# A retention layer and a leaky-ReLU MLP on one core: one load handed from GpSimd to SyncE, a smaller limit on GpSimd's loads under way, and two pairs of casts placed ahead of later loads

## The chip, the core and the metric

The kernel runs on one core of a Trainium2 chip. The time is device microseconds of one launch, from a median of eight runs; lower is better. One further execution was taken with the hardware profiler, and every duration below comes from that one.

## What is computed

The first stage is causal retention over a batch of 8, 8 heads, 576 positions and a head size of 64, and the second is a two-layer MLP on its output. The reference, cut to what matters:

```python
scores = scale * np.matmul(q, k.transpose(0, 1, 3, 2))
Dmat = np.where(rel >= 0, gamma ** rel, 0.0)        # per head, rel = i - j
ret = np.matmul(scores * Dmat, v)
x = ret.transpose(0, 2, 1, 3).reshape(4608, 512)    # tokens x model
h = x @ w_in                                        # 512 x 2048
out = np.maximum(0.01 * h, h) @ w_out               # 2048 x 512
```

All inputs and the output are float32; the kernel multiplies in float16 and accumulates in float32.

## The kernel before

**Units.** The 4608 tokens are cut into 36 units of 128 tokens (two chunks of 64). For each unit the kernel loads q, k and v (256 KB each; three tags of a pool with five buffers, `t32_0`, `t32_1`, `t32_2`), casts them to float16, transposes q and k, multiplies k by q and k by v per head (`scores`, L209), masks (`masks`, L232), carries a running state in float32 (`states`, L241), and puts together the unit's output (`outputs_acc`, L280, for units 0 to 3; `outputs`, L313, after that) in `xT`. A load of a unit that spans two batch entries is two transfers of 128 KB (unit 4 is one).

**Who casts.** `cast_k` (L155) is on ScalarE. `scaled` (L159) puts q and v on VectorE for units 0 to 5 and on GpSimd from unit 6 on. From unit 7 on (`NPE = 7`) `cast_q` also has SyncE issue a DMA transpose of the cast q and k (L171); before that TensorE transposes (`transposes`, L187).

**MLP.** The tokens of two units make a group g. Its first layer is eight blocks of eight 256-column matmuls (L455), each block followed by a leaky ReLU on ScalarE (L462) that frees one of two PSUM buffers `hps`. The second layer is 512-column matmuls (L523 for groups 0 and 1 together, the "wide" blocks; L478 afterwards). VectorE or ScalarE copies the result to one of four buffers `osb`, and SyncE stores it (L490, L534).

**Order.** Each engine runs its instructions in program order; the order is written by hand from L543 to L656, then the units go on as `steps` of the loop (`steady`, L406), spread between the blocks of the MLP by `run` (L498). In `steady(n)` SyncE loads unit n+6 and unit n+3 is cast. Up to unit 11 the loads are issued by GpSimd, except k and q of unit 0, which SyncE issues. So GpSimd's queue holds, in this order: v of unit 0, units 1 to 3, the eight halves of `w_in` (512 KB in HBM each, cast to float16 by the DMA), `w_out` quarter 0 (1 MB in HBM), unit 4, `w_out` quarter 1, unit 5, `w_out` quarters 2 and 3, units 6 to 9, casts of unit 6, load of unit 10, casts of unit 7, load of unit 11, casts of units 8 to 11.

**The limit.** `ring` (L128) keeps a list of GpSimd's transfers with their size in HBM. Before a transfer that would bring the listed sum over `RING` (13 x 256 KB), GpSimd copies one element of the oldest listed transfer's destination into a scratch tile (`probe`, L132); this copy waits for that transfer to land, and GpSimd waits with it. Apart from that, the framework gives GpSimd's DMAs eight completion semaphores in turn, and the ninth DMA waits on the first's; the DMAs of SyncE and ScalarE together have eight more, used the same way.

Names used below: k10 is the load of k of unit 10; T7 is SyncE's DMA transpose for unit 7; w_out(2) is the third quarter of `w_out`.

Of the kernel before, what the change touches and what calls it, by code (L numbers as in the profile page):

```python
# [17 lines left out]
def kernel(  # L18
# [23 lines left out]
    nc = tc.nc  # L42
# [7 lines left out]
    NF = DFF // P  # L50
    TOK = 512
    XR = NT // 2
    RING = 13 << 18

    gamma = 1.0 - 2.0 ** (-5.0 - np.arange(H, dtype=np.float64))
    scale = 1.0 / np.sqrt(D)
# [71 lines left out]
    def ring(size, at):  # L128

        while landing and sum(n for n, _ in landing) + size > RING:  # L130
            x = landing.pop(0)[1]
            nc.gpsimd.tensor_copy(out=probe[0:1, 0:1], in_=x)  # L132
        landing.append((size, at))
# [4 lines left out]
    def load(u, x, eng):  # L138
        t = ld_pool.tile([P, H, D], FP, name=f"t32_{x}")
        t32[u, x] = t  # L140
        (b0, c0), (b1, c1) = units[u]
        src = (q, k, v)[x]
        parts = [(t, b0, c0, P)] if b0 == b1 else [(t[0:CH], b0, c0, CH), (t[CH:P], b1, c1, CH)]
        for dst, b, c, n in parts:
            if eng is nc.gpsimd:
                ring(H * n * D * 4, dst[0:1, 0, 0:1])
            eng.dma_start(  # L147
                out=dst, in_=src[b, :, CH * c : CH * c + n, :].rearrange("h t d -> t h d")
            )

    def loads(u, eng):
        for x in (1, 0, 2):
            load(u, x, eng)

    def cast_k(u):  # L155
        qk16[u] = b_pool.tile([P, 2, H, D], F16, name="qk16")
        nc.scalar.copy(out=qk16[u][:, 1], in_=t32[u, 1])  # L157
# [9 lines left out]
    def cast_q(u):  # L167
        scaled(u, 0, qk16[u][:, 0])
        if u >= NPE:
            qkT[u] = b_pool.tile([P, 2, NP, P], F16, name="qkT")  # L170
            nc.sync.dma_start_transpose(  # L171
                out=qkT[u].rearrange("p x c t -> p (x c) t"),
                in_=qk16[u].rearrange("t x h d -> t (x h d)"),
            )

    def cast_v(u):
        v16[u] = b_pool.tile([P, H, D], F16, name="v16")
        scaled(u, 2, v16[u])

    def casts(u):  # L180
        if u >= NU:
            return
        cast_k(u)
        cast_q(u)
        cast_v(u)

    def transposes(u, pool=None):  # L187

        qkT[u] = b_pool.tile([P, 2, NP, P], F16, name="qkT")
        if pool is None:  # L190
            trs = [y_pool.tile([P, NP, P], F16, name="yps") for x in range(2)]
        else:
            both = pool.tile([P, 2, 2 * NP, P], F16, name="sc" if pool is sc_pool else "ot")
            trs = [both[:, x, 0:NP, :] for x in range(2)]
        for x in (1, 0):
            for p in range(NP):
                nc.tensor.transpose(
                    trs[x][:, p, :],
                    qk16[u][:, x, 2 * p : 2 * p + 2, :].rearrange("t h d -> t (h d)"),
                    ident,  # L200
                )
        for x in (1, 0):
            (nc.scalar.copy if x or u < 4 else nc.vector.tensor_copy)(
                out=qkT[u][:, x], in_=trs[x]
            )
# [185 lines left out]

    load(0, 1, nc.sync)
    load(0, 0, nc.sync)
    load(0, 2, nc.gpsimd)
    for u in (1, 2, 3):
        loads(u, nc.gpsimd)
    for c in range(4):
# [200 lines left out]
    def some(a, b):  # L598
        for m in range(a, b):
            wide[m]()  # L600
# [3 lines left out]
    def more(blocks, a, b):  # L604
        for m in range(a, b):
            blocks[m]()
# [15 lines left out]
    states(5)  # L622
    loads(9, nc.gpsimd)
    casts(6)
    some(9, 12)
    loads(10, nc.gpsimd)
    casts(7)
    some(12, 13)
    outputs(5)
    some(13, 16)  # L630
    more(g1[2], 0, 1)
    transposes(6, sc_pool)
    loads(11, nc.gpsimd)
    casts(8)
    more(g1[2], 1, 3)
    scores(6)
    masks(6)
# [67 lines left out]
```

## Time and profile before

| | us |
|---|---|
| median of 8 runs | 306.11 |
| lowest and highest run | 303.77, 307.25 |
| the profiled execution | 306.61 |
| its span, first to last instruction | 304.7 |
| TensorE busy | 291.7 (96%) |
| ScalarE, GpSimd, VectorE busy | 138.0, 123.2, 107.0 |

The profiled execution is 1.9 us longer than its span, and 0.5 us longer than the median of the runs. The page of the profile gives the busy share of each engine in 40 slices of 7.6 us, the groups of instructions, the DMA queues (q0 is GpSimd's, q1 is SyncE's), and the chain of work that ended last, followed back from the end. The timeline of an engine lists its instructions with start, duration and the idle time ahead of each, with what ended that idle time.

### The profile page before, as it was taken

How to read it: one execution, taken by the hardware profiler on the slowest of the kernel's cores; microseconds unless marked ns; L12 is line 12 of the kernel's file. 1: busy time of each engine (PE TensorE's matmuls, PEld its weight loads, DVE VectorE, ACT ScalarE, POOL GpSimd, SP SyncE). 2: the span in 40 equal slices, each digit the busy share in tenths (PEclk: the TensorE clock that was granted, in tenths of full speed). 3: DMA queues.
4: the chain of work that ended last, by engine and by line, in shares of the span. 5: the costliest groups of instructions: out<-in, count | busy, mean ns of one | idle time of the engine just before them, and what ended most of it. 6: DMA issues, size and time to landing. Idle time of an engine off the chain costs nothing.

```text
span 304.7 us, 9480 instructions
## 1 busy us (share of the span) xinstructions
PE 291.7 (96%) x4169; PEld 197.2 (65%) x4169; DVE 107.0 (35%) x200; ACT 138.0 (45%) x240; POOL 123.2 (40%) x177
## 2 busy tenths in 40 slices
PE   3989999998899999999999999999999999999996
PEld 3467755846666666666666666666666666666663
DVE  2760144344442425242524243433333234331001
ACT  3676634844554445353535353535353534343320
POOL 8986989972533333333333333333333330000000
PEclk9999999999999999999999999999999999999999
DMA  8999998998899999968496957685797221000111
GB/s 223 262 189 238 203 253 268 226 197 197 195 205 199 263 212 198 199 168 199 131 183 163 216 141 177 169 184 160 156 174 189 73 69 39 34 37 34 39 66 69
DMA packets 120440, 50.26 MB, mean 165 GB/s; under 512 B 109264, under 2 KB 113744, under 8 KB 120400
## 3 DMA queue, kind: packets, MB, share of 16 engines
q1 hardware_dynamic: 112912, 36.38, 54.0%
q0 software_dynamic: 7056, 13.11, 18.4%
q8 instruction: 32, 0.52, 0.8%
q10 hardware_dynamic: 432, 0.17, 0.3%
q14 instruction: 8, 0.07, 0.1%
HBM read 36.81 MB, written 9.44 MB: 152 GB/s over the span
## 4 chain that ended last, share of the span: by engine, by line
PE 71%; DMA 12%; POOL 9%; issue 4%; SPq 2%; ACT 0%; POOLq 0%; ACTq 0%
PE yps L478 33%; PE hps L455 32%; DMA w_out<-in_moe_w_out_dram 5%; POOL t L147 5%; DMA t<-in_v_dram 3%; PE sc L216 2%; DMA w_in<-in_moe_w_in_dram 2%; DMA qkT<-qk 2%; POOL probe L132 1%; SPq L147 1%; PE ot L323 1%; PE yps L665 1%; PE ot L334 1%; DMA t<-in_k_dram 1%; PE sc L225 1%
## 5 line engine op out<-in xcount | busy, mean ns | idle before, releaser
L455 PE MATMUL hps<-xT,w_in 128*128 128x256 f16 x1152 | 146.2, 273 | 2.5 <-ACT gt L462 1.4
L462 ACT ACTIVATE gt<-hps 128x512 f16<-128x512 f32 x144 | 85.7, 597 | 125.9 <-PE hps L455 125.6
L455 PEld LDWEIGHTS <-w_in 128*128 128x128 f16 x1152 | 112.1, 98 | 40.7 <-issue 3.1
L478 PE MATMUL yps<-w_out,gt 128*128 128x512 f16 x496 | 126.3, 380 | 0.0
L268 POOL CAST st<-s 128x512 f16<-128x512 f32 (+1 forms) x28 | 15.6, 557 | 138.5 <-DVE s L255 54.9
L478 PEld LDWEIGHTS <-gt 128*128 128x128 f16 x496 | 46.3, 98 | 34.3
L346 DVE TENSOR_TENSOR xT<-ot,own 128x512 f16<-128x512 f32 x32 | 22.1, 692 | 80.0 <-ACT own L342 80.0
L488 DVE COPY osb<-yps 128x512 f32<-128x512 f32 x31 | 21.3, 687 | 75.4 <-PE yps L478 75.4
L160 POOL TENSOR_TENSOR v<-t,cs 128x512 f16<-128x512 f32 x30 | 31.3, 1042 | 1.2 <-DMA t<-in_v_dram 1.2
L160 POOL TENSOR_TENSOR qk<-t,cs 128x512 f16<-128x512 f32 x30 | 31.3, 1043 | 0.7 <-DMA t<-in_q_dram 0.5
L234 DVE TENSOR_TENSOR s<-sc,cs 128x512 f16<-128x512 f32 x36 | 24.6, 683 | 8.2 <-PE sc L225 8.2
L157 ACT CAST qk<-t 128x512 f16<-128x512 f32 x36 | 22.2, 621 | 5.3 <-DMA t<-in_k_dram 5.3
L342 ACT COPY own<-ot 128x512 f32<-128x512 f32 x32 | 18.8, 586 | 7.1 <-PE ot L334 5.2
L255 DVE TENSOR_TENSOR s<-sc,s 128x256 f32<-128x256 f32 x40 | 16.8, 420 | 0.7
L216 PEld LDWEIGHTS <-qkT 64*64 64x64 f16 x576 | 7.8, 108 | 11.9 <-issue 7.3
L216 PE MATMUL sc<-qkT 64*64 64x64 f16 x576 | 11.6, 199 | 2.4 <-DVE s L255 1.2
L147 POOL DMA_DIRECT2D t<-in_v_dram x13 | 11.3, 868 | 1.0 <-POOLq L689 0.8
L147 POOL DMA_DIRECT2D t<-in_k_dram x12 | 10.4, 865 | 1.7 <-ACT gt L462 1.7
L225 PE MATMUL sc<-v,qk 64*64 64x64 f16 x576 | 10.9, 194 | 0.1
L147 POOL DMA_DIRECT2D t<-in_q_dram x12 | 10.2, 853 | 1.2 <-DMA t<-in_k_dram 1.2
L523 PEld LDWEIGHTS <-gt 128*128 128x128 f16 x64 | 5.9, 98 | 6.3
L323 PE MATMUL ot<-s,v 64*64 64x64 f16 x512 | 9.8, 194 | 0.0
(52 smaller groups left out, 145.4 us busy)
## 6 DMA issues: line engine op xcount, KB each, us to landing
out_dram<-osb SPq DMA_DIRECT2D x35, 256.0 KB, 3.8
t<-in_k_dram SPq DMA_DIRECT2D x22, 256.0 KB, 3.6
t<-in_q_dram SPq DMA_DIRECT2D x22, 256.0 KB, 4.1
t<-in_v_dram SPq DMA_DIRECT2D x21, 256.0 KB, 4.5
t<-in_v_dram POOLq DMA_DIRECT2D x11, 256.0 KB, 5.4
t<-in_k_dram POOLq DMA_DIRECT2D x10, 256.0 KB, 4.9
t<-in_q_dram POOLq DMA_DIRECT2D x10, 256.0 KB, 5.4
w_in<-in_moe_w_in_dram POOLq DMA_DIRECT2D x8, 256.0 KB, 6.1
```

The costliest lines, as they stand in the source:

```text
L147: eng.dma_start(out=dst, in_=src[b, :, CH * c : CH * c + n, :].rearrange("h t d -> t h d"))
L157: nc.scalar.copy(out=qk16[u][:, 1], in_=t32[u, 1])
L160: (nc.vector if u < NEARLY else nc.gpsimd).tensor_tensor(out=out, in0=t32[u, x], in1=tab_sb[:, kind(u), x // 2, :].unsqueeze(2).to_broadca ...
L216: nc.tensor.matmul(out=a[half(j), g, 0, p, :], lhsT=qkT[u][half(g), 1, p, half(j)], rhs=qkT[u][half(g), 0, p, half(j)], start=True, stop=T ...
L234: nc.vector.tensor_tensor(out=s16s[u], in0=sc_tiles[u][:, :, 0], in1=mask_sb.unsqueeze(1).unsqueeze(1).to_broadcast([P, 2, NP, CH]), op=MUL,)
L255: nc.vector.tensor_tensor(out=dst, in0=st[:, j], in1=prev, op=ADD)
L342: nc.scalar.copy(out=tmp.rearrange("q c (j t) -> q c j t", t=CH), in_=own.rearrange("q j c t -> q c j t"),)
L346: nc.vector.tensor_tensor(out=xT[:, :, t0 : t0 + P].rearrange("q (s g) t -> q g s t", g=2), in0=far, in1=tmp.rearrange("q (s g) t -> q g s ...
L455: nc.tensor.matmul(out=hps[:, f, :], lhsT=w_in16[:, c, fc * P : (fc + 1) * P], rhs=xT[:, c, t0 % XR : t0 % XR + tok], start=(c == 0), stop ...
L462: nc.scalar.activation(out=g_tiles[g][:, fb * nf : (fb + 1) * nf, :], in_=hps, func=mybir.ActivationFunctionType.Lrelu,)
L478: nc.tensor.matmul(out=y_cur[g, tb], lhsT=g_tiles[g][:, f, tb * P : (tb + 1) * P], rhs=w_out16[:, f, :], start=(f == 0), stop=(f == NF - 1),)
L488: nc.vector.tensor_copy(out=osb, in_=y_cur[g, tb])
```

## The change

There are three edits. `RING` goes from 13 to 10 times 256 KB. The load of v of unit 0 is issued by SyncE, after k and q of the same unit, and is no longer in GpSimd's list. The casts of unit 7 stand ahead of the load of unit 10, and the casts of unit 8 ahead of the load of unit 11.

```diff
-    RING = 13 << 18
+    RING = 10 << 18
...
     load(0, 1, nc.sync)
     load(0, 0, nc.sync)
-    load(0, 2, nc.gpsimd)
+    load(0, 2, nc.sync)
...
     loads(9, nc.gpsimd)
     casts(6)
+    casts(7)
     some(9, 12)
     loads(10, nc.gpsimd)
-    casts(7)
     some(12, 13)
...
     transposes(6, sc_pool)
+    casts(8)
     loads(11, nc.gpsimd)
-    casts(8)
     more(g1[2], 1, 3)
```

The order of instructions on TensorE, VectorE and ScalarE is the same in both kernels. On SyncE one load is added in the third place. On GpSimd the first load is gone, the probes stand in other places, and eight instructions (four casts, with the loads around them) change places.

## The prediction

> **What bounds the kernel now.** I read the page's slices first, then the list of TensorE's waits, then the timelines of SyncE and GpSimd where those waits fall.
>
> ```profile
> span 304.7 us, 9480 instructions
> PE 291.7 (96%) x4169; PEld 197.2 (65%) x4169; DVE 107.0 (35%) x200; ACT 138.0 (45%) x240; POOL 123.2 (40%) x177
> ...
> PE   3989999998899999999999999999999999999996
> ...
> POOL 8986989972533333333333333333333330000000
> ...
> DMA  8999998998899999968496957685797221000111
> ```
>
> TensorE is full from slice 11 (84 us) to the end, and GpSimd works hard in the first 12 slices alone. Whatever the change does, it does it before about 88 us; after that TensorE runs on at its own pace and the end moves as that point moves. So the sum is a shift of TensorE's work at 80 to 88 us. What TensorE waits for:
>
> ```profile
> PE yps L197 <- DVE qk L160: 1.7, 1, 1.7
> PE yps L197 <- ACT qk L157: 1.6, 1, 1.6
> PE hps L455 <- ACT gt L462: 1.4, 2, 1.1
> PE hps L387 <- DVE idle L375: 1.4, 1, 1.4
> PE sc L216 <- DVE s L255: 1.2, 1, 1.2
> PE hps L455 <- issue: 1.1, 1, 1.1
> PE sc L216 <- ACT qkT L203: 0.7, 1, 0.7
> PE sc L216 <- DMA qkT<-qk: 0.5, 1, 0.5
> ```
>
> The columns are the total, the count and the longest. 6.5 us of this lies before 25 us (k0, q0, the start, one issue gap, unit 2's transposes). Between 60 and 80 us there are four waits of 3.0 us in all: 0.32 at 60.28 (ScalarE's leaky ReLU), 0.48 at 68.33 (T8), 1.16 at 74.33 (VectorE's state of unit 9) and 1.07 at 79.02 (a leaky ReLU that stands behind ScalarE's cast of k13, which waits for that load). The last one ends last. The chain of waits leads from it to k13's load (issued 74.40, landed 77.70), and from there back along SyncE's queue:
>
> ```profile
> 54.72 1.32 SPq L171 DMA_TRANSPOSE qkT<-qk  x1
> 56.08 3.02 SPq L534 DMA_DIRECT2D out_dram<-osb  x4
> 59.76 10.04 SPq L171 DMA_TRANSPOSE qkT<-qk  x4
> 69.92 0.51 SPq L147 DMA_DIRECT2D t<-in_k_dram  x1
> ```
>
> The columns are the start and the duration. T7 waits for GpSimd's cast of q7 (53.63 to 54.68). The four stores stand behind it, though the first one's data was ready at 49.92. T8 starts as q8's cast ends (59.74); then T8 to T11 follow each other with no gap (2.91, 2.95, 2.06, 1.63 us) and the loads of units 12 and 13 come behind them. So what counts is **when T11 leaves SyncE**: 68.18. The chain puts GpSimd's cast of v11 ahead of it, but T10 and T11 need the casts of q10 and q11 only, which were done at 63.7 and 65.7; SyncE was simply busy.
>
> **Edit 1, v0 on SyncE.** GpSimd's first issue (1.24 to 2.29) goes, and its next loads start 1.05 earlier. SyncE issues v0 at about 1.8, behind q0. q0's last packets ran at 5.56. SyncE's packets are 256 B and take 18 ns each, 14 ns apart; a DMA engine has 64 of them per load, 0.9 to 1.15 us (GpSimd's packets are 4096 B in 160 ns, 0.64 us per load). So v0's data ends at 6.5 to 6.8 and lands at 6.9 to 7.2, where it landed at 6.62. VectorE casts it behind q0 (from 6.95 to 7.64) and TensorE uses it at 8.72: 1.1 us of cover for at most 0.6 of delay. Cost 0. Without that cover each microsecond would be one of TensorE's. It gains nothing either: the waits before 25 us are on k0 and q0, whose rivals on the DMA engines stay (GpSimd's first load still starts at 1.24).
>
> The row that speaks for this: in the packets of before, one DMA engine sent 46 of q0's 256 B packets 14 ns apart from 4.91 to 5.56, while one 4096 B packet of GpSimd's queue stretched there from 0.16 to 0.88 us. The Trainium skill speaks against it: "DMA: Bandwidth & Descriptors", section "Queues, rings and completion order", says that an engine goes round its queues and changes at every packet. By that, each of v0's packets would wait for one of 4096 B, and v0 would land near 16; the row says that it doesn't.
>
> **Edit 2, the limit of 10 x 256 KB.** Among plain loads it changes nothing, since eight semaphores already keep eight loads (2 MB) under way. It bites around the weights:
>
> ```profile
> 37.58 0.89 POOL L147 DMA_DIRECT2D t<-in_v_dram  x1
> 38.46 0.17 POOL L132 COPY probe<-t 1x1 f32<-1x1 f32 x1
> 38.58 0.88 POOL L147 DMA_DIRECT2D t<-in_k_dram  x1
> 39.45 0.67 POOL L132 COPY probe<-t 1x1 f32<-1x1 f32 x1
> 40.07 0.88 POOL L147 DMA_DIRECT2D t<-in_q_dram  x1
> 40.95 0.17 POOL L132 CAST probe<-w_out 1x1 f32<-1x1 f16 x1
> 41.10 0.89 POOL L147 DMA_DIRECT2D t<-in_v_dram  x1
> ```
>
> The probe at 40.95 is that of w_out(2), which landed at 40.51. Before, it stands ahead of v7, so v6, k7 and q7 are already issued. With the smaller limit it stands ahead of v6. So GpSimd is at 40.7 with ten loads to issue up to v9, where it had seven: 10 x 0.88 and four probes of 0.13 give 50.0, against 48.71 before, when it also stood 1.25 idle at 44.10 for the last quarter of w_out. The earlier delays by the same rule (w_out(1) issued after w_out(0)'s landing at 28.83, about 29.2 for 26.66; w_out(2) about 1 later) leave the DMA engines fed or nearly so, and w_out(2) lands at 40.5 to 41. I take **+1.5 us**, casts of unit 6 from 50.2. Bounds: 0 if w_out(2) lands by 39, +2.3 if it lands past 41. Cover: TensorE's transposes of unit 6 are at 52.97 and need q6 cast, then 51.2; all weights land over 2 us before use.
>
> **Edit 3, the casts.** GpSimd's order becomes casts 6, 7, load 10, casts 8, load 11, casts 9, 10, 11. A pair of casts takes 2.0 us, three loads with probes 3.0:
>
> - q7 cast at 53.3 (before 54.7), T7 and the four stores 1.4 earlier;
> - load 10 from 54.3 (50.70): k10 lands 3.6 to 4.5 later, 57.9 to 58.8; ScalarE casts it at 59.11. Covered, by 0.3 at worst;
> - q8 cast at 58.3, T8 then (59.76): 1.4 earlier, so it should land before 67.85, and the wait of 0.48 goes;
> - load 11 from 59.2 (55.74): k11 took 4.39 before, so 63.6; ScalarE casts it at 63.86 and has until 64.6;
> - casts of q9, q10, q11 end at 63.3, 65.3, 67.3 (61.7, 63.7, 65.7): 1.5 later.
>
> So T9 now waits for GpSimd, not for SyncE: 63.3 against 62.84. With the durations of before T10 and T11 follow at 66.3 and 68.4 (+0.2); with T7's 1.32 each T11 starts at 67.3 (-0.9). The DMA work is the same and a little more spread, so I take a third of that way: **T11 at 67.9, -0.3**. The loads of units 12 and 13, k13's cast and TensorE at 79.02 move with it. Delays from k10 or k11 up to about 1 us end in the same 1.07 us wait and are swallowed; the 1.16 for VectorE is a chain of its own and stays.
>
> **Sum.** 0 - 0.3 on the profiled 306.61 (span 304.7 and 1.9 around it) gives 306.3. That execution is 0.5 above the median of the runs, so the forecast for the median is **305.8 us**. That is no change: 0.5%, 1.5 us, is about what a measurement of this kernel can tell.
>
> **Rivals.**
>
> *GpSimd becomes the bound (slower).* The load of q11 is issued at 60.2 and took 6.55 before; v11 took 8.05. At 8.05 q11 lands at 68.3, T11 leaves at 69.4 (+1.2); with w_out(2) late as well, GpSimd is 0.8 later still and T11 leaves at about 70.1: +1.9, of which nothing is swallowed, since it comes by k13 itself. 308.0. It decides from the point where q11's cast ends after 68.2. For it: in this stretch stores and transposes fill the DMA engines. Against it: the stores are out 1.4 earlier.
>
> *The queue of SyncE clears (faster).* If w_out(2) lands by 39 (its 1 MB took 5.1 us beside 2.6 for the quarter after it), GpSimd is not late, q11's cast ends at 65.8, and the transposes shorten to 1.3: T11 at 66.5, -1.7. TensorE can follow by 1.55, the 1.07 and the 0.48 that it waits. 306.6 - 1.55 - 0.5 = 304.5. Against it: the limit delays GpSimd in any case by three loads against the wait of 1.25.
>
> *v0 starves behind GpSimd's packets (slower).* 64 turns of 178 ns from 4.4 are 15.8; v0 lands at 16.2 and TensorE starts 8.2 late, less some 2 us of later waits: 312. The row of 46 packets speaks against it.
>
> *The change does not do what it says:* excluded for the casts and the load by the order of instructions; for the limit it is the case in which only load slots bind, and the sum is then the second rival's.
>
> **How the numbers follow.** Forecast (between 304.8 and 307.0) 0.50, GpSimd the bound 0.25, the faster case 0.20, starving 0.05. The range from 304.2 to 308.4 takes in the first three with their bounds and leaves out starving and the ends. Faster by over 0.5% 0.20, slower by over 0.5% 0.29, within 0.51 (a little of the slower rival ends below the half percent, and some of the forecast's case above it).
>
> **What would show it.** Right: v0 lands at about 7 and TensorE's first 25 us don't move; the casts of unit 6 start at 49.5 to 51; T7 at about 53.3, T8 at 58.3; T9 follows q9's cast at once; T11 at 67.3 to 68.6; no wait for T8 at 68; the wait near 79 is there, 0.3 smaller by the clock. Wrong: v0 after 8 us; ScalarE idle for k10 at 59 or for k11 over 1 us at 64; T11 past 69.4; a shift that arises before 25 us or after 90.

## The result, and the profile after

The changed kernel takes **308.79 us** (median of 11 runs, 306.31 to 313.01); the kernel before, run beside it, 305.48 (32 runs). The ratio is **1.009 [1.006, 1.012]**: slower by more than half a percent, where the forecast was no change, and 0.4 us above the range given. The profiled execution of the changed kernel took 310.07 (span 308.2), that of before 306.61 (304.7), so 3.5 us are to be found.

The page of the changed kernel, the lines that answer to those shown of before:

```profile
span 308.2 us, 9489 instructions
PE 292.9 (95%) x4169; PEld 198.1 (64%) x4169; DVE 107.3 (35%) x200; ACT 138.0 (45%) x240; POOL 121.7 (39%) x178
...
PE   5789999887899999999999999999999999999996
...
POOL 8757779983453333333333333333333330000000
PEclk9999999997999999999999999999999999999999
DMA  8999899798899995967596966777797220000012
```

TensorE is full from the twelfth slice on, as before. The loss lies ahead of that: slices 8 to 11 (54 to 85 us) read 8, 8, 7, 8, and in the tenth the granted clock dropped, which it nowhere did in the profile of before. TensorE's waits in the changed kernel (total, count, longest):

```profile
PE hps L455 <- DVE xT L346: 3.3, 1, 3.3
PE sc L225 <- DVE v L160: 1.8, 1, 1.8
PE yps L197 <- ACT qk L157: 1.4, 1, 1.4
...
PE yps L197 <- DVE qk L160: 0.8, 1, 0.8
PE hps L455 <- ACT gt L462: 0.6, 1, 0.6
PE sc L197 <- POOL qk L160: 0.4, 1, 0.4
PE sc L216 <- DMA qkT<-qk: 0.3, 1, 0.3
```

The first line is new and is the largest of all. The second, for the cast of v0, is new too. The 1.1 us that stood last before (the leaky ReLU near 79) is gone.

Where the two executions part is read by setting the start of the same `scores` on TensorE side by side:

| scores of unit | before | after | after minus before |
|---|---|---|---|
| 4 | 40.32 | 39.82 | -0.50 |
| 6 | 55.26 | 55.37 | +0.11 |
| 7 | 59.50 | 60.11 | +0.61 |
| 8 | 68.33 | 72.91 | +4.58 |
| 10 | 74.33 | 79.29 | +4.96 |
| 12 | 87.86 | 91.42 | +3.56 |
| 20 | 149.40 | 153.02 | +3.62 |

So TensorE is half a microsecond ahead at unit 4, then 1.1 are lost around the transposes of units 6 and 7, 4 between units 7 and 8, and 1.4 come back before unit 12. From there on nothing changes. The lead at unit 4 can't be put down to the change: in the fourteen profiles of this case these `scores` start between 38.48 and 42.11 us, and before, at 40.32, is the latest but one.

The 4.0 us between units 7 and 8 go through ScalarE. Its timeline in the changed kernel (start, duration, and in brackets the idle time ahead):

```profile
59.96 0.62 ACT L157 CAST qk<-t 128x512 f16<-128x512 f32 x1 [0.64 <-DMA t<-in_k_dram]
...
69.23 0.62 ACT L157 CAST qk<-t 128x512 f16<-128x512 f32 x1 [4.43 <-DMA t<-in_k_dram]
69.76 0.58 ACT L342 COPY own<-ot 128x512 f32<-128x512 f32 x1
```

The second cast is that of k11. ScalarE stands 4.43 us for this load, and behind the cast stands the copy for `xT` of unit 7, which TensorE needs next: it waits 3.29 us and starts again at 71.11. The same place on TensorE, before and after:

```profile
66.81 1.04 PE L455 MATMUL hps<-xT,w_in 128*128 128x256 f16 x8
68.33 0.32 PE L216 MATMUL sc<-qkT 64*64 64x64 f16 x16 [0.48 <-DMA qkT<-qk]
...
71.11 1.86 PE L455 MATMUL hps<-xT,w_in 128*128 128x256 f16 x8 [3.29 <-DVE xT L346]
72.91 0.43 PE L216 MATMUL sc<-qkT 64*64 64x64 f16 x16
```

Then comes something no theory of mine had. TensorE's clock by stretches (columns: length, busy time of PE, PEld, DVE, ACT, POOL, granted clock, DMA share, GB/s):

```profile
68.00:70.60 2.60, 0.00 (x0) 0.00 (x0) 0.23 (x1) 1.10 (x2) 0.71 (x2) 1.00 1.28 124
70.60:74.00 3.40, 2.89 (x43) 1.89 (x43) 0.86 (x2) 0.60 (x1) 1.65 (x2) 0.50 0.90 196
74.00:76.00 2.00, 2.00 (x64) 1.26 (x66) 1.15 (x3) 0.60 (x1) 0.40 (x1) 1.00 0.97 220
```

At 70.60, near the end of the wait, the granted clock falls to 0.50, and it is 1.00 again at 74.02: 3.41 us at half speed. The step between units 7 and 8 is 3.97 us (4.58 - 0.61). It is made up of the wait of 3.29; 0.76, since the eight matmuls at 71.11 hold the next ones up for 1.80 us where it was 1.04 before; and 0.25 more of the wait for a leaky ReLU at 61.13 (0.57 for 0.32); less the 0.48 for T8 that is no longer waited for. That is 3.82; the other 0.15 I can't place.

Why k11 was late is on GpSimd. Before, the second and third quarter of `w_out` were issued, and q6 was cast, at these times (same columns as ScalarE's timeline):

```profile
26.66 0.78 POOL L365 DMA_DIRECT2D w_out<-in_moe_w_out_dram  x1 [0.70 <-issue]
...
32.91 0.76 POOL L365 DMA_DIRECT2D w_out<-in_moe_w_out_dram  x1
...
48.71 1.05 POOL L160 TENSOR_TENSOR qk<-t,cs 128x512 f16<-128x512 f32 x1
```

In the changed kernel (the lines with w_out are probes and loads of its quarters):

```profile
29.75 0.17 POOL L132 CAST probe<-w_out 1x1 f32<-1x1 f16 x1 [1.43 <-DMA w_out<-in_moe_w_out_dram]
30.20 0.77 POOL L365 DMA_DIRECT2D w_out<-in_moe_w_out_dram  x1 [0.28 <-issue]
...
36.34 0.17 POOL L132 CAST probe<-w_out 1x1 f32<-1x1 f16 x1 [0.78 <-DMA w_out<-in_moe_w_out_dram]
36.80 0.76 POOL L365 DMA_DIRECT2D w_out<-in_moe_w_out_dram  x1 [0.28 <-issue]
...
42.50 0.17 POOL L132 CAST probe<-w_out 1x1 f32<-1x1 f16 x1 [1.52 <-DMA w_out<-in_moe_w_out_dram]
42.97 0.89 POOL L147 DMA_DIRECT2D t<-in_v_dram  x1 [0.29 <-DVE qkT L203]
...
52.18 1.05 POOL L160 TENSOR_TENSOR qk<-t,cs 128x512 f16<-128x512 f32 x1
...
61.34 0.92 POOL L147 DMA_DIRECT2D t<-in_k_dram  x1
```

This is a chain. The quarters' landings are 29.62, 36.22 and 42.38, and each probe runs within 0.13 us of one. Behind the first probe w_out(1) is issued, behind the second w_out(2), behind the third v6. One link takes 0.45 us from probe to issue and 6.0 or 5.6 from issue to landing. GpSimd casts q6 at 52.18, where it was 48.71 before: 3.5 us late. The rest of its queue follows with the durations of before. k11's load is issued at 61.34 instead of 55.74, 5.6 us late: the 3.5, and 2.1 for the casts of unit 8 that now stand ahead of it (edit 3). It lands at 69.16.

SyncE is late too, T7 by 0.5 us, T8 by 0.7 and T11 by 3.1; its timeline after:

```profile
55.25 2.40 SPq L171 DMA_TRANSPOSE qkT<-qk  x1
57.70 2.53 SPq L534 DMA_DIRECT2D out_dram<-osb  x4
60.41 12.10 SPq L171 DMA_TRANSPOSE qkT<-qk  x4
72.62 0.52 SPq L147 DMA_DIRECT2D t<-in_k_dram  x1
```

T11 leaves at 71.28 (68.18 before), since GpSimd's cast of q11 begins at 70.21. But TensorE, itself late by then, no longer waits for what hangs on it.

### The profile page after: what moved, and what is told of

It is laid out like the page before. It is cut to its first block, busy times and chain, and to the rows that moved or that the text cites. A ratio compares the mean times of both kernels' runs of the same rounds, so it can differ in the third digit from the quotient of the medians.

```text
span 308.2 us, 9489 instructions
## 1 busy us (share of the span) xinstructions
PE 292.9 (95%) x4169; PEld 198.1 (64%) x4169; DVE 107.3 (35%) x200; ACT 138.0 (45%) x240; POOL 121.7 (39%) x178
## 4 chain that ended last, share of the span: by engine, by line
PE 84%; POOL 5%; DMA 5%; DVE 2%; issue 1%; ACT 1%; SPq 0%; POOLq 0%; ACTq 0%
PE hps L455 39%; PE yps L478 34%; POOL t L147 3%; PE sc L216 3%; DMA t<-in_k_dram 3%; DMA t<-in_v_dram 2%; PE sc L225 2%; PE ot L334 1%; PE ot L323 1%; PE yps L665 1%; POOL qk L160 1%; POOL v L160 1%; PE yps L523 1%; PE hps L381 1%; DVE s L234 1%
## 5 line engine op out<-in xcount | busy, mean ns | idle before, releaser
L147 POOL DMA_DIRECT2D t<-in_v_dram x12 | 10.2, 850 | 0.3 <-DVE qkT L203 0.3
L268 ACT CAST st<-s 128x512 f16<-128x512 f32 (+1 forms) x8 | 4.8, 596 | 11.1 <-DVE s L255 7.5
```

What stands on the lines that cost most here:

```text
L147: eng.dma_start(out=dst, in_=src[b, :, CH * c : CH * c + n, :].rearrange("h t d -> t h d"))
L268: (nc.scalar.copy if u < NACT else nc.gpsimd.tensor_copy)(out=st16[u][:, js], in_=st32[u][:, js])
```

## The experiments

Every kernel was timed in five rounds against the kernel before on the same chip (6 runs each of e1 and e4, 12 of each of the others); the ratios are to that, with a 95% interval. Before had 305.10 beside the first four, 305.72 beside the next four, 305.01 beside e9 to e11 and 305.06 beside e12. The theories after the result:

- **A**: the loss is ScalarE's wait for k11, and needs the smaller limit and the moved casts together.
- **B**: the limit alone makes GpSimd late, and TensorE meets that in whatever of GpSimd's products is due next.
- **C**: v0 on SyncE comes late and holds TensorE up at the start.
- Later **D** (v0 on SyncE spoils what the other edits bring), **E** (fewer bytes under way leave the DMA engines without work anywhere, not just at `w_out`) and **F** (a limit is needed: without one GpSimd's loads harm others).

### One edit at a time: e1, e2, e3

e1 is the kernel before with the limit alone, e2 with v0 on SyncE alone, e3 with the moved casts alone.

```diff
-    RING = 13 << 18
+    RING = 10 << 18
```

> The limit of 10 x 256 KB alone. Theory A (the loss is k11 landing after 64.6 us, where ScalarE's cast of it holds up the output of unit 7; it takes the limit's delay and the moved casts together): GpSimd's casts of unit 6 start at 51 to 52 instead of 48.7, load 11 is issued at about 58.5 instead of 55.7, k11 lands at 63 to 65, ScalarE idles for it under 0.5 us, ratio 1.000 to 1.003. Theory B (GpSimd late by the limit is the loss by itself, through T9 to T11 and the loads of units 12 and 13): ratio 1.006 or more, with no long idle time of ScalarE. Theory C (the loss is v0's late landing at the start): ratio 1.000.

```diff
-    load(0, 2, nc.gpsimd)
+    load(0, 2, nc.sync)
```

> v0 on SyncE alone. Theory A: v0 lands at 8 to 9 us, TensorE waits about 1.8 us for its cast and is 0.8 us late at 9.5 us, and that is swallowed by later waits before 80 us; ratio 0.999 to 1.002. Theory B: ratio 1.000. Theory C: ratio 1.006 or more.

```diff
+    casts(7)
     some(9, 12)
     loads(10, nc.gpsimd)
-    casts(7)
...
+    casts(8)
     loads(11, nc.gpsimd)
-    casts(8)
```

> The moved casts alone. Theory A: load 11 is issued 2 us later than before, at about 57.8, k11 lands at 62 to 64 within ScalarE's slack, T8 lands earlier; ratio 0.997 to 1.001. Theory B: ratio 0.996 to 1.000, since T7 and T8 come earlier. Theory C: ratio 1.000.

Measured: e1 310.19 us, **1.015 [1.010, 1.020]**; e2 304.13, **0.998 [0.995, 1.000]**; e3 305.79, **1.002 [0.998, 1.005]**. The limit alone loses at least as much as the whole change (the intervals overlap a little); C falls; A falls as the sole cause, since e1 has no moved casts and k11 lands there 4.31 us after its issue. In e1 the chain of quarters is the same (w_out(1) issued at 32.04, w_out(2) at 38.39, cast of q6 at 54.32), but TensorE waits elsewhere:

```profile
PE sc L216 <- DMA qkT<-qk: 3.3, 2, 1.9
...
PE sc L197 <- POOL qk L160: 1.1, 1, 1.1
```

Here the late products are the transposes T7 and T8 (3.3 us) and the cast of q6 itself (1.1), not k11. That is B. In e2 v0 lands at 7.83, and TensorE waits 0.5 us for its cast, less than the 1.8 that I expected from the changed kernel. e3 shows the other side: GpSimd is on time (q6 at 48.48), but k10 and k11 need 6.96 and 9.59 us to land (k11 at 67.10, where 62 to 64 was expected), and TensorE waits once for a leaky ReLU that stands behind ScalarE's cast of k10:

```profile
PE hps L455 <- ACT gt L462: 2.1, 1, 2.1
```

### The wait for k11 taken away: e4 and e11

e4 is the changed kernel with the cast of k11 on GpSimd instead of ScalarE; e11 loads k11 ahead of the casts of unit 8, with q11 and v11 behind them.

```diff
-        nc.scalar.copy(out=qk16[u][:, 1], in_=t32[u, 1])
+        (nc.gpsimd.tensor_copy if u == 11 else nc.scalar.copy)(
+            out=qk16[u][:, 1], in_=t32[u, 1]
+        )
```

> The changed kernel, with the cast of k of unit 11 taken from ScalarE and put on GpSimd, ahead of its cast of q11 (0.56 us more of GpSimd). Theory A: ScalarE's 4.4 us of idle time at 65 to 69 us and TensorE's wait of 3.3 us at 71 us go; what is left is T8 to T11 and the loads of units 12 and 13, some 2 us later than before; ratio to the kernel before 1.004 to 1.007, about 1 us better than the changed kernel (1.009). Theory B: no better than the changed kernel, 1.009 to 1.011. Theory C: 1.009.

```diff
+    load(11, 1, nc.gpsimd)
     casts(8)
-    loads(11, nc.gpsimd)
+    load(11, 0, nc.gpsimd)
+    load(11, 2, nc.gpsimd)
```

> The changed kernel with one load moved back: k of unit 11 is loaded ahead of the casts of unit 8, q and v of unit 11 stay behind them. It takes away ScalarE's wait for k11 and nothing else. Theory A (that wait, with TensorE's wait of 3.3 us and the half clock after it, carries the loss of the changed kernel): k11 lands by 65.5, the wait of 3.3 us near 71 is gone or under 1.3 us, no half clock; ratio 0.998 to 1.004. Theory B (the late GpSimd carries it, and another of its products is late next: the transposes T9 to T11 and the load of k13 stay as late as they are): ratio 1.004 to 1.010, with the waits moved to the transposes or to the cast of k13.

e4: 308.61, **1.010 [1.004, 1.017]**. e11: 307.63, **1.007 [1.004, 1.010]**. The wait of 3.3 us is gone in both, the loss is not, or hardly. e4's interval also holds the 1.004 to 1.007 that A gave it; e11 is the one that speaks against A, which gave it 0.998 to 1.004. The waits of e11 (in its profiled execution the matmuls ran at half their later speed until 21.7 us, in that of the changed kernel until 12.6, so I use its waits and not its times):

```profile
PE hps L455 <- ACT gt L462: 3.3, 3, 1.3
```

Three waits of 1.34, 1.01 and 0.94 us, behind ScalarE's casts of k10, k12 and k13, add up to what the one wait for k11 was. e4 has the same three places with 0.94, 0.92 and 1.02. The lateness is GpSimd's, and taking away one product that meets it lets the next one meet it.

### Pairs: e5 and e8

e5 has the limit and v0, without the casts; e8 has v0 and the casts, with the limit of before.

> The limit and v0 on SyncE, without the moved casts. Theory B, now sharper (under the limit each quarter of w_out waits for the landing of the one before, so that GpSimd reaches the casts of unit 6 some 3.5 to 5.5 us late and T7 and T8, behind the load of unit 10, come too late for TensorE): casts of unit 6 at 52 to 53.5, T7 at 58 to 59.5, TensorE waits for T7 or T8; ratio 1.010 to 1.014. Theory A (the loss needs the moved casts too): ratio 1.000 to 1.003, already unlikely after the limit alone. Theory D (v0 on SyncE is what spoils it, by its late landing beside the limit): ratio above 1.015.

> v0 and the moved casts with the old limit, so the change without its first edit. Theory B: the limit is the whole loss; ratio 0.997 to 1.002, and k10, issued behind the casts of unit 7, may hold ScalarE up by 0 to 2 us as with the moved casts alone. Theory A (moved casts make k10 and k11 late): ratio 1.003 to 1.006.

e5: 308.53, **1.007 [1.004, 1.011]**; e8: 304.63, **0.999 [0.996, 1.002]**. Without the limit of 10 there is no loss, with it there is, whether or not the casts are moved; D falls. e5's cast of q6 comes at 50.59 and T7 at 56.74, earlier than expected, and its ratio is below the 1.010 to 1.014 that B gave it. In e1, without v0 on SyncE, q6 was cast at 54.32 and the ratio is 1.015: under the limit edit 1 seems to give something back, though the two intervals just overlap. e5 too waits for transposes and not for k11:

```profile
PE sc L216 <- DMA qkT<-qk: 3.4, 3, 1.9
```

### Which property of the limit: e6 and e9

e6 is the changed kernel with each quarter of `w_out` put on the list with 512 KB instead of its 1 MB. e9 is the changed kernel with a limit of 11 x 256 KB.

```diff
-        ring(P * 4 * DM * 4, w_out16[0:1, 4 * c, 0:1])
+        ring(P * 4 * DM * 2, w_out16[0:1, 4 * c, 0:1])
```

> The changed kernel, all three edits kept, but a quarter of w_out counts in GpSimd's list with 512 KB, its size in SBUF, instead of 1 MB. No quarter then waits for the quarter just before it. Theory B: casts of unit 6 start at 47 to 48.5 instead of 52.2, k11 lands by 64 and ScalarE idles for it under 1 us; ratio 0.997 to 1.002. Theory E (any smaller number of bytes under way starves the DMA engines, w_out or not): ratio 1.006 or more.

```diff
-    RING = 10 << 18
+    RING = 11 << 18
```

> The changed kernel with a limit of 11 x 256 KB in place of 10 x 256 KB. Theory B in its sharp form (the sum 1.0 + 0.75 + 1.0 MB = 2.75 MB, which 10 x 256 KB does not hold and 11 x 256 KB just holds, puts each quarter of w_out behind the landing of the quarter before it): w_out(1) is issued near 26 again instead of 30.2, w_out(2) near 33 instead of 36.8, the cast of q6 starts at 48 to 49.5 instead of 52.2, no wait of TensorE for k11's cast over 1 us; ratio to before 0.996 to 1.002. Rival (the loss grows gradually as the limit shrinks, so one 256 KB step gives back about a third of it): w_out(1) near 28.5, cast of q6 near 51, ratio 1.005 to 1.008.

e6: 304.93, **0.997 [0.994, 1.000]**. Its limit is 10 x 256 KB everywhere else, so E falls; undoing the chain of quarters undoes the loss. Its smaller numbers missed a little: q6 is cast at 48.74, k11 lands at 65.05 and ScalarE stands 1.01 us for it. e9: 306.18, **1.001 [0.997, 1.004]**. One step of 256 KB takes nearly the whole loss away, as the sum says: a quarter (1.0 MB), three loads (0.75) and the next quarter (1.0) are 2.75 MB, which 11 x 256 KB holds and 10 x 256 KB does not. Three numbers of my expectation missed: w_out(1) is issued at 26.90, about as expected, but w_out(2) at 35.24 (33 expected), q6 is cast at 49.80, and a long wait behind k11's cast is left. In e9's trace the load of k5 still waits for w_out(0), and six probes of unit 4 (1.35 us) stand ahead of w_out(2):

```profile
30.05 0.17 POOL L132 CAST probe<-w_out 1x1 f32<-1x1 f16 x1 [2.37 <-DMA w_out<-in_moe_w_out_dram]
31.11 0.92 POOL L147 DMA_DIRECT2D t<-in_k_dram  x1 [0.88 <-ACT gt L462]
...
33.77 1.35 POOL L132 COPY probe<-t 1x1 f32<-1x1 f32 x6
35.24 0.76 POOL L365 DMA_DIRECT2D w_out<-in_moe_w_out_dram  x1
```

So a softer form of the same chain remains, and k11 (7.5 us to land) still costs TensorE 2.4 us in that profile.

### No limit that binds: e7, e10, e12

`RING` is 64 x 256 KB: in e7 with v0 on SyncE, in e10 with nothing else changed from before, in e12 with v0 and the moved casts. The list reaches this sum only at the last loads, where one or two probes look at transfers that landed long before.

```diff
-    RING = 13 << 18
+    RING = 64 << 18
```

> v0 on SyncE and no limit (64 x 256 KB, never reached; eight semaphores still hold GpSimd to eight transfers under way). Theory B: the limit only ever delays GpSimd; casts of unit 6 at 46 to 47.2 (47.25 with v0 alone), ratio 0.994 to 0.998. A rival (F: more bytes under way delay w_in and the loads that TensorE needs first, and the stores and transposes beside them): ratio 0.998 to 1.004.

> The kernel before with a limit so large that it never binds (64 x 256 KB in place of 13 x 256 KB); v of unit 0 stays on GpSimd, no cast is moved. It splits what the version with both v of unit 0 on SyncE and no limit gained (0.996). Theory B with an additive gain: v on SyncE alone was 0.998, so the limit's share is about 0.002: ratio 0.996 to 1.000, cast of q6 near 48 instead of 48.7. Rival (a limit is needed, since GpSimd's loads otherwise crowd the first units' loads on the DMA engines): the first 25 us get longer by 1 us or more, ratio over 1.003.

> The changed kernel with a limit so large that it never binds (64 x 256 KB in place of 10 x 256 KB): v of unit 0 on SyncE and the moved casts stay. If the limit is the whole of the loss (theory B), the time falls to that of the versions without a limit, 0.995 to 0.999 of before, with the cast of q6 near 47. What the moved casts are worth once GpSimd is early: in the kernels with them, k10 and k11 landed 6 to 10 us after their issue in most profiles instead of 3.6 to 4.6. If that decides, ScalarE waits for one of the two and the version stays 0.002 or more above the one without moved casts (0.996); if not, it is the same as that one or faster, since the transposes of units 7 and 8 leave SyncE 1 to 1.5 us earlier.

e7: 303.87, **0.996 [0.993, 0.999]**; e10: 304.03, **0.997 [0.994, 1.001]**; e12: 304.10, **0.9968 [0.9940, 0.9996]**. F falls: nothing gets slower, and GpSimd is early (q6 cast at 47.05, 46.76, 46.93). It still waits for landings without a probe, 1.93 us ahead of a load at 39.76 in e7, by its eight completion semaphores. What F feared is seen once, and costs nothing in the end: in e10 TensorE waits 1.39 us for `w_in` at 18.16, but `scores` of unit 4 start at 39.35, earlier than before (40.32). The three cannot be told apart; e7 and e12 are faster than the kernel before, by intervals that end just short of no difference. With an early GpSimd the moved casts show no gain at the end: e12 sends T11 off at 64.13, e7 at 65.43, and yet `scores` of unit 12 start at 85.03 and 85.21. TensorE's waits in e12 between 55 and 90 us are the two that remain when nothing is late:

```profile
PE sc L216 <- DVE s L255: 1.2, 1, 1.2
...
PE hps L455 <- ACT gt L462: 0.3, 1, 0.3
```

## Why the prediction was wrong

**The step that failed is the size of edit 2**: "w_out(2) about 1 later" and, from it, "**+1.5 us**, casts of unit 6 from 50.2". I let the rule act once, on w_out(1), and left w_out(2) 1 us behind its old place. By the same sum w_out(2) has to wait for the landing of w_out(1), and v6 for that of w_out(2). What I put at 29.2, 33.9 and 40.7 (w_out(1), w_out(2), GpSimd free for v6) was 30.20, 36.80 and 42.97. Of the 1.0 that w_out(1) is off, 0.8 come from ahead of it: w_out(0) was issued 2.2 us later than before (22.49 for 20.25), behind probes for the halves of `w_in`, and landed 0.8 later. From v6 on the count held: ten loads with probes took 9.2 us (9.3 counted). So q6 was cast 3.5 us late instead of 1.5, outside the bounds of 0 to 2.3 too. e1, e6 and e9 show that this is the limit and that it hangs on that sum.

**Edit 3** had the right order and spacing. From the cast of q6 on, T7, load 10, T8 and load 11 were put 3.1, 4.1, 8.1 and 9.0 us behind; they came 3.07, 4.11, 8.23 and 9.16 behind. All of it was 2 us late because of edit 2. One duration was wrong: k11 was given 4.39 us to land and took 7.82. The runs make this a regular thing: in the eight kernels with the moved casts k11 took 6.3 to 9.6 us, in the six without them 4.2 to 4.9. There, k11 is issued 4 us before T8 and is nearly down when T8 starts; with the casts moved the two are issued within 2 us. That T8's packets hold k11's up is a guess: no run separated T8 from the four stores ahead of it, so it stays open which of them does. ScalarE was ready for k11 at 64.8: with the old 4.39 us the late issue alone would have let it stand 0.9 us, with the landing of 7.82 alone, on the issue at 59.2, 2.2 us; together they made 4.43.

**Edit 1** was priced at 0 by a step that was wrong: v0 was to land at 6.9 to 7.2 within a cover of 1.1 us. It landed at 8.78 (7.5 to 8.2 in the other kernels with this edit), and TensorE waited 1.8 us for its cast; at the `scores` of units 1 to 3 it stood 0.8 us later than before. That the price came out near 0 all the same is luck. A gap of 1.14 us on TensorE near 23 us in the profile of before, whose cause the profile doesn't name, was not there after the change; but it is missing too in e1 and e3, which keep v0 on GpSimd. And q0 landed 1.2 us earlier than before (5.08 for 6.24), but so it did with v0 on GpSimd in e1 (5.04) and e10 (5.08). That it "gains nothing either" may be slightly off: GpSimd casts q6 1.5 us earlier in e2, and e2 is at 0.998 [0.995, 1.000].

Starving did not come. In the packets of the changed kernel all but 69 of v0's 1024 pieces of 256 B started by 6.5 us, as put; most of the rest ran 14 ns apart from 6.72 to 7.47, four came 0.17 to 0.20 us apart, and the last started at 8.28. The Trainium skill ("DMA: Bandwidth & Descriptors", section "Queues, rings and completion order") has a DMA engine drain a whole packet, typically some 9 to 17 descriptors and at most 64, before it turns to another queue. I had taken each piece of 256 B for such a packet; the 16 us come from that reading, and the page doesn't say it.

**The 1.07 us near 79** was swallowed as said, and the 0.48 for T8 went. **The half clock** at the wait was not in the sum at all.

**The rivals.** "GpSimd becomes the bound" (308.0, chance 0.25) was the one that came true in its condition: T11 left past 69.4. Its path did not: I let the lateness come by q11, T11 and k13, and TensorE met it before that, at k11. I had written down "ScalarE idle for k11 over 1 us at 64" as a sign against the forecast; it was the sign that appeared. Had the chain been priced, T11 at 67.9 would have stood about 2 us later, past that rival's 69.4, and about its 308.0 would have been the forecast; that the measured 308.79 is near it is in part luck, since the path was another and half the runs have the half clock (see below).

## What to carry to other kernels

When a limit on bytes makes the issuer wait for its oldest transfer, run its list by hand through every large transfer: if two neighbours and what lies between them do not fit, the transfers become a chain, and each link costs a whole latency (6 us here), not a share of bandwidth. Count such a delay through every later product of that queue, and do not expect much from removing the one that a profile shows waiting, as e4 and e11 show. A load that is moved next to another queue's transfers keeps its issue cost but not its landing time; give it the longest landing seen in such a neighbourhood.

## What the runs showed of the hardware

**A wait of TensorE can cost more than itself.** Beside the wait of 3.3 us here, and within 1.3 us after waits of 2.1 in e3, 1.9 in e5 and 1.8 in e6, the granted clock fell to 0.50 for 3.41 us, then was 1.00 again. One such drop makes an execution's mean clock 0.994, which each run reports, so that they can be counted: 6 of the changed kernel's 11 runs have a mean clock of 0.994 or less (median 309.8; the other five 307.9). Of the 104 runs of the kernel before in the experiments it is 22, and in each of the four batches these are 1.5 to 3.1 us longer in the median than the rest; in e2, e7, e8 and e12 it is none of 48, in e11, without the long wait, 2 of 12.

What brings a drop about is not settled. The profiles of e2, e7, e8 and e12 show no wait over 1.3 us after 15 us, but those of before and of e4 (2 of 6 runs) don't either. Length alone doesn't decide: in e9 a wait of 2.4 us and in e1 one of 1.9 were followed by no drop, while the clock of e1 fell at 15.30 us, where the longest wait in the 9 us before was 0.97 and TensorE had been busy for 2.17 of the last 3.42 us. The Trainium skill, "TensorE: Matmul & The Clock Gate", section "Why this matters for your kernels", names gaps over about 3 us for this; here waits of 1.8 to 2.1 us came just ahead of a drop in three profiles. Its section "Part 1: The HAM clock gate" describes a free-running window of about 3.4 us; the 3.41 us agree with that, and whether the place of the window decides is not shown here.

**The time is then a mixture.** A change that makes such drops likelier can move the median by more than its own delay, and it widens the spread: e12's 12 runs, none with a drop, lie within 1.6 us, those of the changed kernel within 6.7.
